# Retention and a squared-ReLU feed-forward net on one core: A11's square on ScalarE, w_out's sums stored in smaller pieces, and transfers held back ahead of the retention products

## The chip, the core and the metric

The kernel runs on one core of a Trainium2 chip, in float32. The metric is device time in microseconds. A core has TensorE (PE in the profile; its weight loads are a row of their own, PEld), VectorE (DVE), ScalarE (ACT), GpSimd (POOL) and SyncE (SP), whose queue issues nearly all transfers here. The engines run their own instruction streams in order and meet at semaphores.

## The reference

```python
q, k, v: (8, 8, 576, 64)           # batch, heads, sequence, head size
scores = q @ k^T / sqrt(64)
Dmat[h, i, j] = gamma[h] ** (i - j) if i >= j else 0
x = ((scores * Dmat) @ v)           # then (batch, seq, heads*64) = (4608, 512)
h = relu(x @ w_in)                  # w_in (512, 2048)
out = (h * h) @ w_out               # w_out (2048, 512), out (4608, 512)
```

The weights may come in as 64-bit floats; the kernel then takes them apart with integer operations on VectorE and ScalarE and puts float32 values together (it calls this rounding).

## The kernel before, in words

**Three strands.** The retention runs over 36 chunks of 128 tokens. The first FFN product runs over 9 blocks of 512 tokens, and its steps are woven between the retention's matmuls. When both are through, a last stage computes the second FFN product from what the first one wrote to DRAM. This last stage is the second part of the span, from about 554 us on.

**The FFN products are done with seven instead of eight block products** (the Strassen-Winograd scheme, `PRODUCTS`, L27). For the first product a block n > 0 has four groups `mp` of seven steps j = 0 to 6, one product each, in `ffn_in` (L723). The products add up in three PSUM banks: h_a (j = 0, 3), h_b (j = 1, 4, 6), h_c (j = 2, 5). A step has four matmuls of 128x128 weights by 256 columns (eight records each of matmuls and weight loads in the trace), and then an ACT or DVE operation that takes the sum out of PSUM:

- j = 0: ACT copies the sum (L748); j = 1 and 2: DVE adds (L750, L752)
- j = 3: ACT applies Relu and makes A11 (L754); POOL multiplies A11 by itself (L755)
- j = 4, 5, 6: DVE adds (L757, L761, L764) and squares (`square`, L745), which makes A22, S3 and A12

A bank that is still read cannot be written, so the matmuls of j = 4 wait for L750, and those of j = 6 for L757. Five results of each group (A11, S1, A12, S3, A22, 256 KB each) go to `g_dram` (`g_store`, L670): A11 in j = 5, A22 in j = 6, and then from a queue of small jobs (`g_sums`, L673, worked off by `some`) A12 in j = 6, S1 and S3 in the next group's j = 0 and 1.

**The retention products** of a chunk are issued by `whole` (L612): 64x64 matmuls, up to 128 of them, that take 2.0 to 2.1 us. They need the transposed q and k of the chunk, which DVE makes block by block (`flip`, L402) and ACT copies in place in 16 small copies (`move`, L421), q scaled (L385) and v scaled (L489) by POOL, and the running state, which ACT copies out of PSUM (L495). After `whole`, the loads of q, k and v for later chunks are issued on SP (`loads`, L867, L155 and L157), and `ffn` (L825) runs the next FFN steps until the pace of a table (`PACE`) is met: seven steps for one chunk in most of the kernel, so that a chunk with its seven steps takes about 14.4 us and its retention products follow j = 6. In `ffn`, `count` is the number of steps still to come before the next retention products. Its flags `held` (the last step) and `busy` (a flip is still to be issued) hold jobs back.

**w_out's preparation** rides along. `w_out_parts` (L259) is a generator of small jobs: 16 pieces of w_out (512 KB each) are fetched (`fetch_w`, L203, three ahead), rounded (`round_parts`, L210: L219, L223 on DVE, L227, L228 on ACT, then L231, L234, L237 on DVE), and summed for the seven products (`right_sums`, L252). A set of sums covers two buffers, `stage[0]` (1.79 MB) and `stage[1]` (1.34 MB), and is stored to `w2_dram` in two transfers (L290). That happens four times. `ffn_in` takes one or two jobs in a step (L780 to L787), at a rate that has all done before block 7 ends; the counter `n_w2` is compared with the steps done.

**The last stage** (from L1138) reads `g_dram` and `w2_dram` back and does the second product block by block, 128x128 matmuls of 128 columns (L1076). Two of its preparations (L1012, L1027 to L1030) run on DVE during the last steps of the first product.

What sets the order around the change is written out by hand: the order of emission is the order of each engine's queue. SP takes transfers strictly in that order, and a transfer whose data is not ready holds up those behind it.

Of the kernel before, what the change touches and what calls it, by code (L numbers as in the profile page):

```python
# [12 lines left out]
AF = mybir.ActivationFunctionType  # L13
ALU = mybir.AluOpType
# [26 lines left out]
def kernel(  # L41
# [33 lines left out]
    nc = tc.nc  # L75
# [8 lines left out]
    N_DF = d_ff // 128  # L84
# [125 lines left out]
    def round_parts(j):  # L210
        words = raw_of(j).bitcast(U32).rearrange("p (n two) -> p n two", two=2)
        lo, hi = words[:, :, 0], words[:, :, 1]
        frac = raw_of(j).rearrange("p (n two) -> p n two", two=2)[:, :, 0]
        exp = exp_of(j).bitcast(U32)
        t = piece_dst(j)
        bits = t.bitcast(U32)

        def one():
            nc.vector.tensor_scalar(exp, hi, 20, 0x7FF, op0=ALU.logical_shift_right, op1=ALU.bitwise_and)  # L219

        def two():

            nc.vector.tensor_scalar(bits, as_dst(j, hi), 0xFFFFF, 0x100000, op0=ALU.bitwise_and, op1=ALU.bitwise_or)  # L223

        def beside():

            nc.scalar.activation(frac, lo, AF.Copy, scale=2.0 ** -52)  # L227
            nc.scalar.activation(exp, exp, AF.Relu, bias=exp_bias[:, 0:1], scale=2.0 ** 23)  # L228

        def three():  # L230
            nc.vector.scalar_tensor_tensor(t, bits, 2.0 ** -20, as_dst(j, frac), op0=ALU.mult, op1=ALU.add)  # L231

        def four():
            nc.vector.tensor_tensor(t, t, as_dst(j, exp_of(j)), op=ALU.mult)  # L234

        def five():
            nc.vector.scalar_tensor_tensor(bits, as_dst(j, hi), 0x80000000, bits, op0=ALU.bitwise_and, op1=ALU.bitwise_or)  # L237

        if not wide:
            to = t if pieces[j][0] == 0 else t.rearrange("p o s f -> p (o s) f")  # L240
            return [lambda: nc.sync.dma_start(to, piece_src(j))] + [lambda: None] * 5
        return [one, two, beside, three, four, five]
# [16 lines left out]
    def w_out_parts():  # L259

        for j in range(N_W1, N_W1 + 3):
            yield lambda j=j: fetch_w(j)
        for j in range(N_W1 + 1, len(pieces), 2):

            pair = [round_parts(j - 1), round_parts(j)]
            for one, two, beside, *_ in pair:
                yield one
                yield two, beside
            for i, (_, _, _, three, four, five) in zip((j - 1, j), pair):
                yield three  # L270
                yield four

                def last(i=i, five=five):
                    five()
                    fetch_w(i + 3)

                yield last
            wi, m, e = pieces[j]
            mh, mq = divmod(m, N_MQ)
            if e == 1:  # L280

                at = slice(2 * mh, 2 * mh + 2)
                b = [stage[0][:, o, at, :] for o in range(4)] + [stage[1][:, o, at, :] for o in range(3)]
                r1, r2, r3, r4 = right_sums(*b)
                yield from (r1, r2, r3, r4)
            if e == 1 and mh == 1:

                for st_, at in ((stage[0], slice(0, 4)), (stage[1], slice(4, 7))):
                    yield from right_sums(*(st_[:, :, o, :] for o in range(NP)))
                    yield lambda st_=st_, at=at, mq=mq: nc.sync.dma_start(  # L290
                        w2_dram[at, :, mq, :].rearrange("o p f -> p o f"), st_.rearrange("p o s f -> p o (s f)"))

    n_made = [0]
    n_raw = [0]
# [428 lines left out]
    def ffn_in(n, mp, j):  # L723

        if j == 0 and mp == 0:

            if n not in sums_x:
                sums_x[n] = sum_x(n)
            for f in sums_x[n]:
                f()  # L730
        left, right, to = PRODUCTS[j]
        if j in OPENS:
            sums[to] = ps_f.tile([128, 2, HT], F32, tag="f", name=f"h_{to}")
        p = sums[to]
        for mm in range(2):
            w = w_in[mp][:, mm, WI_SLOT[left], :, :]
            for c in range(2):
                nc.tensor.matmul(p[:, mm, :], lhsT=w[:, c, :], rhs=xs[n][right][:, c, :],  # L738
                                 start=(j in OPENS and mm == 0 and c == 0), stop=(j in CLOSES and c == 1),
                                 skip_group_check=True)  # L740
        g = g_of(mp)
        p1, u2, p15 = (p_room[mp % 2][:, s, :, :] for s in range(3))

        def square(t):
            nc.vector.scalar_tensor_tensor(t, t, 0.0, t, op0=ALU.max, op1=ALU.mult)  # L745

        if j == 0:
            nc.scalar.copy(p1, p)  # L748
        elif j == 1:
            nc.vector.tensor_tensor(u2, p, p1, op=ALU.add)  # L750
        elif j == 2:
            nc.vector.tensor_tensor(p15, p, p1, op=ALU.add)  # L752
        elif j == 3:
            nc.scalar.activation(g["A11"], p, AF.Relu)  # L754
            nc.gpsimd.tensor_tensor(g["A11"], g["A11"], g["A11"], op=ALU.mult)  # L755
        elif j == 4:
            nc.vector.tensor_tensor(g["A22"], p, p15, op=ALU.add)  # L757
            square(g["A22"])
        elif j == 5:

            nc.vector.tensor_tensor(g["S3"], p, u2, op=ALU.add)  # L761
            square(g["S3"])
        else:
            nc.vector.tensor_tensor(g["A12"], p, p1, op=ALU.add)  # L764
            square(g["A12"])
            queue.extend(g_sums(n, mp))

        if j in (5, 6):
            g_store(n, mp, "A11" if j == 5 else "A22")

        if mp == N_MP - 1 and j in (3, 4, 5) and n_next[0] > n + 1:
            if n + 1 not in sums_x:
                sums_x[n + 1] = sum_x(n + 1)
            sums_x[n + 1].pop(0)()
        if j in (6, 0, 1, 2, 3):
            some(2 if n == 1 and mp == 0 else 1)
        if n == 1 and 1 <= j < 5 and mp + 1 < N_MP:
            sums_w.setdefault(mp + 1, sum_w_in(mp + 1)).pop(0)()

        late_w2 = 0.92 * (done[0] - N_0) - n_w2[0]  # L780
        for _ in range(0 if busy[0] else 2 if late_w2 > 1.5 and j in (0, 3) else late_w2 > 0):
            if not (held[0] and type(w_out_next[0]) is tuple):
                n_w2[0] += 1
                f = w_out_next[0]
                w_out_next[0] = next(w_out_steps, None)
                for f in f if type(f) is tuple else (f,):
                    f and f()  # L787
        if n == N_BLK - 2 and mp == 3 and j in (0, 3):
            assert w_out_next[0] is None
            fetch_w2(j // 3)  # L790
# [4 lines left out]
    w_out_steps = w_out_parts()  # L795
    w_out_next = [next(w_out_steps)]
    held = [False]
    busy = [False]
    n_w2 = [0]

    def block_steps(n):
# [2 lines left out]
            return seconds + [(0, first_in, j) for j in range(N_HALF, N_W1)]  # L804
        return [(n, ffn_in, n, mp, j) for mp in range(N_MP) for j in range(NP)]

    def step():
        n, f, *args = steps.pop(0)
        done[0] += 1
        f(*args)  # L810

    n_next = [0]
    n_scaled = [N_EARLY + 2]
# [11 lines left out]
    def ffn(i, half):  # L825

        gone[0] += C if half == 2 else C / 2
        if steps and steps[0][0] == 0:

            move(6)  # L830
            for _ in range(2 if half and i > N_EARLY else 1):
                if steps and steps[0][0] == 0:
                    convert(6)
                    step()
            return
        if not behind:
            behind.append((gone[0] - HALF, done[0]))
        points = behind + [p for p in PACE if p[0] > behind[0][0]]
        want = points[-1][1]
        for (x0, y0), (x1, y1) in zip(points, points[1:]):  # L840
            if gone[0] < x1:
                want = y0 + (y1 - y0) * (gone[0] - x0) / (x1 - x0)
                break
        count = max(1, int(want) - done[0])
        while steps and count:
            held[0] = half != 1 and count <= (1 if half else 2)

            if half == 2:
                due = sum(m[0] <= i + 2 for m in moves)
                move(max(2, min(4, -(-due // (count - 1)))) if count > 1 else 0)  # L850
            else:
                move(4 if half and len(moves) > 8 else 3 if half else 2 if count > 1 else 0)
            busy[0] = len(flips) > 0
            for f in flips[:1]:
                f()
            del flips[:1]
            step()
            count -= 1
        held[0] = busy[0] = False


    def warm(count):
# [364 lines left out]
```

## Time and profile before

| | |
|---|---|
| median of 3 runs | 954.22 us (953.71 to 954.39) |
| profiled execution | 954.21 us, span of its instructions 952.5 us |
| PE busy | 940.9 us, 99% of the span |
| DVE busy | 777.9 us, 82% |
| ACT busy | 344.0 us, 36%, nearly all of it before 480 us |
| POOL busy | 126.9 us, 13%; L755 has 34.7 of them, L489 51.6, L385 41.0 |
| DMA | 181.43 MB, 190 GB/s over the span |
| stores of the FFN's results | 164 of 256 KB, 3.9 us from issue to landing (median) |
| stores of w_out's sums | 4 of 1792 KB, 6.7 us, and 4 of 1344 KB, 6.1 us |
| fetches of w_out | 16 of 512 KB, 4.6 us |

In the profile "busy" is the time in which an engine has an instruction under way. Matmuls are pipelined and their ends are modelled, so PE's busy time hides small holes, and the starts of its matmuls tell more. A wait row names the engine and line that waited, then what released it. "issue" stands for time in which an engine waited for nothing that the profile shows. PEclk is the granted clock of TensorE as a share of full speed. The page also lists a queue q8 of the kind "instruction", with 76 packets and 1.25 MB.

### The profile page before, as it was taken

How to read it: one execution, taken by the hardware profiler on the slowest of the kernel's cores; microseconds unless marked ns; L12 is line 12 of the kernel's file. 1: busy time of each engine (PE TensorE's matmuls, PEld its weight loads, DVE VectorE, ACT ScalarE, POOL GpSimd, SP SyncE). 2: the span in 40 equal slices, each digit the busy share in tenths (PEclk: the TensorE clock that was granted, in tenths of full speed). 3: DMA queues.
4: the chain of work that ended last, by engine and by line, in shares of the span. 5: the costliest groups of instructions: out<-in, count | busy, mean ns of one | idle time of the engine just before them, and what ended most of it. 6: DMA issues, size and time to landing. Idle time of an engine off the chain costs nothing. (4 is left out here: it accounts for less than half of the span.)

```text
span 952.5 us, 23368 instructions
## 1 busy us (share of the span) xinstructions
PE 940.9 (99%) x9748; PEld 845.9 (89%) x9748; DVE 777.9 (82%) x1422; ACT 344.0 (36%) x812; POOL 126.9 (13%) x115
## 2 busy tenths in 40 slices
PE   8999999999999999999999999999999999999998
PEld 7655888888888888888888899999999999999998
DVE  5789799879898978888856588888878788787876
ACT  4466667567666665766610000000000000000000
POOL 4223131221231312212100000000000000000000
PEclk9999999999999999999999999999999999999999
DMA  9995667695678755863469984535555453525241
GB/s 221 240 287 145 178 187 191 179 283 153 177 210 263 194 154 170 284 183 103 164 201 362 352 294 146 188 129 171 178 157 189 180 182 135 200 100 177 96 172 45
DMA packets 172778, 181.43 MB, mean 190 GB/s; under 512 B 118784, under 2 KB 133248, under 8 KB 166016
## 3 DMA queue, kind: packets, MB, share of 16 engines
q1 hardware_dynamic: 170576, 179.41, 60.6%
q8 instruction: 76, 1.25, 0.6%
q10 hardware_dynamic: 2096, 0.52, 0.3%
q14 instruction: 30, 0.25, 0.1%
HBM read 109.39 MB, written 70.52 MB: 189 GB/s over the span
## 5 line engine op out<-in xcount | busy, mean ns | idle before, releaser
L738 PE MATMUL h_b<-room,w 128*128 128x256 f32 x768 | 182.2, 380 | 2.2 <-DVE room L757 1.9
L421 ACT COPY qk<-flip 32x256 f32<-32x256 f32 x416 | 167.3, 402 | 6.6
L738 PEld LDWEIGHTS h_b<-room,w 128*128 128x128 f32 x768 | 145.8, 190 | 23.4 <-DVE room L757 2.8
L1076 PE MATMUL o_b<-w,room 128*128 128x128 f32 x1168 | 144.4, 275 | 0.2 <-DVE room L1028 0.2
L1076 PEld LDWEIGHTS o_b<-w,room 128*128 128x128 f32 x1168 | 137.3, 192 | 0.4 <-DVE room L1028 0.4
L738 PE MATMUL h_a<-room,w 128*128 128x256 f32 x512 | 125.6, 388 | 1.7 <-issue 1.7
L1076 PE MATMUL o_c<-w,room 128*128 128x128 f32 x1008 | 123.0, 275 | 0.0
L738 PE MATMUL h_c<-room,w 128*128 128x256 f32 x512 | 121.0, 379 | 0.0
L1076 PEld LDWEIGHTS o_c<-w,room 128*128 128x128 f32 x1008 | 117.7, 192 | 0.0
L1090 ACT COPY r<-o_a 128x128 f32<-128x128 f32 x53 | 14.1, 266 | 271.3 <-PE o_a L1076 235.7
L738 PEld LDWEIGHTS h_a<-room,w 128*128 128x128 f32 x512 | 96.0, 191 | 16.1 <-issue 2.2
L738 PEld LDWEIGHTS h_c<-room,w 128*128 128x128 f32 x512 | 97.3, 190 | 13.2
L1076 PE MATMUL o_a<-w,a 128*128 128x128 f32 x688 | 85.6, 275 | 0.0
L755 POOL TENSOR_TENSOR room<-room 128x512 f32<-128x512 f32 x32 | 34.7, 1086 | 361.5 <-ACT room L754 295.9
L1076 PEld LDWEIGHTS o_a<-w,a 128*128 128x128 f32 x688 | 81.2, 192 | 0.1
L745 DVE SCALAR_TENSOR_TENSOR room<-room 128x512 f32<-128x512 f32 x96 | 73.8, 768 | 3.3
L700 PE MATMUL h_ps<-room,w 128*128 128x512 f32 (+2 forms) x160 | 58.8, 516 | 0.7 <-DVE w L237 0.7
L489 POOL TENSOR_TENSOR v_ld<-v_ld,dv 128x512 f32<-128x512 f32 x36 | 51.6, 1435 | 16.4 <-DMA v_ld<-in_v_dram 16.4
L757 DVE TENSOR_TENSOR room<-h_b,room 128x512 f32<-128x512 f32 x32 | 22.0, 689 | 37.6 <-PE h_b L738 37.6
L597 PEld LDWEIGHTS x_ps<-qk,v_ld 64*64 64x64 f32 x1024 | 38.4, 134 | 12.7 <-issue 11.7
L597 PE MATMUL x_ps<-qk,v_ld 64*64 64x64 f32 x1024 | 48.3, 222 | 0.0
L700 PEld LDWEIGHTS h_ps<-room,w 128*128 128x128 f32 x160 | 27.1, 190 | 23.8 <-issue 21.3
(114 smaller groups left out, 1352.2 us busy)
## 6 DMA issues: line engine op xcount, KB each, us to landing
g_dram<-room SPq DMA_DIRECT2D x164, 256.0 KB, 3.9
a<-g_dram SPq DMA_DIRECT2D x30, 1024.0 KB, 6.1
room<-g_dram SPq DMA_DIRECT2D x15, 1024.0 KB, 6.0
w<-w_dram SPq DMA_DIRECT2D x7, 1792.0 KB, 11.2
out_dram<-room SPq DMA_DIRECT2D x17, 512.0 KB, 3.3
q_ld<-in_q_dram SPq DMA_DIRECT2D x64, 128.0 KB, 4.6
w<-in_moe_w_in_dram SPq DMA_DIRECT2D x16, 512.0 KB, 6.2
w<-in_moe_w_out_dram SPq DMA_DIRECT2D x16, 512.0 KB, 4.6
```

Source lines behind the costliest of these rows:

```text
L421: nc.scalar.copy(*moves.pop(0)[2:])
L489: nc.gpsimd.tensor_tensor(vs, vs, dv[:, :, at:at + 1].to_broadcast([C, H, D]), op=ALU.mult)
L597: return [lambda hp=hp, e=e, b=b: nc.tensor.matmul(x_at(hp, e, b, h), lhsT=s["vs"][rows(h), head(hp, e), :], rhs=s["ret"][rows(h), e, hp, ...
L700: nc.tensor.matmul(p, lhsT=w[:, c, :], rhs=xT[0][:, c, :].rearrange("p (h t) -> p h t", h=2)[:, lo:hi, at[0]:at[1]], start=(c == 0), stop= ...
L738: nc.tensor.matmul(p[:, mm, :], lhsT=w[:, c, :], rhs=xs[n][right][:, c, :], start=(j in OPENS and mm == 0 and c == 0), stop=(j in CLOSES a ...
L745: nc.vector.scalar_tensor_tensor(t, t, 0.0, t, op0=ALU.max, op1=ALU.mult)
L755: nc.gpsimd.tensor_tensor(g["A11"], g["A11"], g["A11"], op=ALU.mult)
L757: nc.vector.tensor_tensor(g["A22"], p, p15, op=ALU.add)
L1076: nc.tensor.matmul(p, lhsT=s["lefts"][left][:, m, :], rhs=w_out[j][:, m, WO_SLOT[right], :], start=(i in OPENS and m == 0), stop=(i in CLO ...
L1090: nc.scalar.copy(r[:, 0, 0:128], p)
```

## The change

- A11's square moves from POOL (in j = 3, right after its Relu) to ACT, as an activation at the start of j = 4's work on ACT.
- A22's store is not issued in j = 6 but put on a list, `transfers`, in j = 5. So is each fetch of w_out that follows the rounding of a piece.
- `step` issues one entry of this list after each step (two, if more than two wait), but only if more than `QUIET = 2` steps are still to come before the next retention products (`ahead`; where none follow, it is large).
- A set of w_out's sums is stored in seven transfers of 458 KB, one for each of the seven products. The first four go out beside the four sums of `stage[1]`; the last three are jobs of a new kind (lists), which take no place in the step's count and wait while `ahead` is 2 or less.

The diff, without the places that only set the new variables up:

```diff
                 def last(i=i, five=five):
                     five()
-                    fetch_w(i + 3)
+                    transfers.append((N_BLK, lambda: fetch_w(i + 3)))
...
-                for st_, at in ((stage[0], slice(0, 4)), (stage[1], slice(4, 7))):
-                    yield from right_sums(*(st_[:, :, o, :] for o in range(NP)))
-                    yield lambda st_=st_, at=at, mq=mq: nc.sync.dma_start(
-                        w2_dram[at, :, mq, :].rearrange("o p f -> p o f"), st_.rearrange("p o s f -> p o (s f)"))
+                def keep(o):
+                    nc.sync.dma_start(w2_dram[o, :, mq, :], stage[o // 4][:, o % 4, :, :].rearrange("p s f -> p (s f)"))
+
+                yield from right_sums(*(stage[0][:, :, o, :] for o in range(NP)))
+                for o, r in enumerate(right_sums(*(stage[1][:, :, o, :] for o in range(NP)))):
+                    yield lambda o=o, r=r: [r(), keep(o)]
+                yield [lambda: [keep(4), keep(5)]]
+                yield [lambda: keep(6)]
...
             nc.scalar.activation(g["A11"], p, AF.Relu)
-            nc.gpsimd.tensor_tensor(g["A11"], g["A11"], g["A11"], op=ALU.mult)
         elif j == 4:
+            nc.scalar.activation(g["A11"], g["A11"], AF.Square)
...
-        if j in (5, 6):
-            g_store(n, mp, "A11" if j == 5 else "A22")
+        if j == 5:
+            g_store(n, mp, "A11")
+            transfers.append((n, lambda: g_store(n, mp, "A22")))
...
-        for _ in range(0 if busy[0] else 2 if late_w2 > 1.5 and j in (0, 3) else late_w2 > 0):
-            if not (held[0] and type(w_out_next[0]) is tuple):
-                n_w2[0] += 1
-                f = w_out_next[0]
-                w_out_next[0] = next(w_out_steps, None)
-                for f in f if type(f) is tuple else (f,):
-                    f and f()
+        count = 0 if busy[0] else 2 if late_w2 > 1.5 and j in (0, 3) else late_w2 > 0
+        while w_out_next[0] and (count or type(w_out_next[0]) is list):
+            f = w_out_next[0]
+            if held[0] and type(f) is tuple or ahead[0] <= QUIET and type(f) is list:
+                break
+            n_w2[0] += 1
+            count -= type(f) is not list
+            w_out_next[0] = next(w_out_steps, None)
+            for f in f if type(f) in (tuple, list) else (f,):
+                f()
+            if type(w_out_next[0]) is list:
+                break
...
     def step():
         n, f, *args = steps.pop(0)
         done[0] += 1
         f(*args)
+        for _ in range(2 if len(transfers) > 2 else 1):
+            if transfers and ahead[0] > QUIET:
+                transfers.pop(0)[1]()
...
+            ahead[0] = count
             busy[0] = len(flips) > 0
```

## The prediction

> **What bounds the kernel now.** I read the page first, then PE's waits, then the order of time around each place where PE's matmul starts lie further apart than usual.
>
> ```profile
> PE 940.9 (99%) x9748; PEld 845.9 (89%) x9748; DVE 777.9 (82%) x1422; ACT 344.0 (36%) x812; POOL 126.9 (13%) x115
> ```
>
> TensorE is busy for 99% of the span. The change touches none of its instructions, so it can win only PE's holes, and lose by making new ones. PE's own waits, named by what ended them (us in total, times, longest):
>
> ```profile
> PE h_b L738 <- DVE room L757: 1.9, 2, 1.5
> PE h_a L738 <- issue: 1.7, 1, 1.7
> ...
> PE sc_ps L471 <- ACT qk L421: 0.5, 1, 0.5
> ...
> PE h_b L738 <- DVE room L750: 0.3, 1, 0.3
> PE o_b L1076 <- DVE room L1028: 0.2, 1, 0.2
> ```
>
> These understate the price, since a matmul's modelled end covers part of a hole. I measured the holes by starts: a step j of the first FFN product follows the last one after 1.73 us, or 1.83 after a break. That gives 0.67 us at 112 us, 1.76 at 140, 0.18 at 217.6, 3.58 at 331 to 338, 0.53 at 457.6, 0.72 at 461.8 and 0.48 at 560: **7.9 us** that this change can reach. The start (0 to 98 us) and the last stage are not touched.
>
> The largest hole, in order of time and as stretches (busy us by engine, then PEclk, DMA share, GB/s):
>
> ```profile
> 326.68 0.33 SPq L205 DMA_DIRECT2D w<-in_moe_w_out_dram  x1
> 327.11 6.71 SPq L671 DMA_DIRECT2D g_dram<-room  x3
> ...
> 331.46 0.48 PE L738 MATMUL h_a<-room,w 128*128 128x256 f32 x1
> ...
> 333.62 3.25 PE L738 MATMUL h_a<-room,w 128*128 128x256 f32 x7 [1.67 <-issue]
> ```
> ```profile
> 331.40:333.60 2.20, 0.54 (x9) 0.19 (x1) 2.17 (x5) 2.06 (x5) 0.00 (x0) 1.00 0.17 44
> 333.60:337.10 3.50, 3.48 (x9) 2.77 (x10) 3.50 (x7) 0.21 (x2) 0.00 (x0) 0.52 0.62 163
> ```
>
> PE waits for nothing that the program knows ("issue"), 1.84 us beyond its pitch. After that the granted clock is 0.52 and eight matmul starts lie about 427 ns apart instead of 216: another 1.74. I explain it by PE's own code. Queue q8 of the page carries 76 packets of 16 KB, one for each 256 of PE's instructions, and one of them starts at 331.23, inside the hole. I counted PE's records (matmuls and weight loads) up to each packet. In the quiet last stage packet k starts at record 256 k + 161, some 0.2 us after record 256 k + 158; I call that record the trigger. Here it passes at 325.56 and the packet starts **5.66 us** later, behind a DMA share over 1. In the last two steps before a retention block this hurts: a step eats 16 instructions in 1.73 us, a block some 256 in 2.1 us. PE ran dry some 287 instructions after the trigger, 5.7 us here.
>
> **Change 1: the square of A11 goes from POOL to ACT.** Removed: 32 POOL multiplies (L755, 1.04 us median, 34.7 busy). They slow VectorE whenever it reads two SBUF tensors at the same time:
>
> ```profile
> 458.08 1.55 POOL L755 TENSOR_TENSOR room<-room 128x512 f32<-128x512 f32 x1 [10.35 <-ACT room L754]
> 458.65 1.26 DVE L254 TENSOR_TENSOR w<-w 128x256 f32<-128x256 f32 x1
> ...
> 459.59 1.23 POOL L489 TENSOR_TENSOR v_ld<-v_ld,dv 128x512 f32<-128x512 f32 x1
> 459.94 1.16 DVE L255 TENSOR_TENSOR w<-w 128x256 f32<-128x256 f32 x1
> 461.03 0.68 DVE L757 TENSOR_TENSOR room<-h_b,room 128x512 f32<-128x512 f32 x1
> ...
> 461.76 1.99 PE L738 MATMUL h_b<-room,w 128*128 128x256 f32 x8 [0.46 <-DVE room L757]
> 462.35 0.42 DVE L256 TENSOR_TENSOR w<-w,w 128x256 f32<-128x256 f32 x1
> ```
>
> L254 and L255 need 0.42 alone (L256 below), so the two lose 1.58 us, L757 comes late and PE waits. POOL's scalings of q and v (L385, L489) stood in POOL's queue behind L755, which waits for ACT's Relu. Without it they run as soon as their loads land. The last v load landed at 440, so around 445 to 448 and 458 to 461 POOL is empty: the holes at 457.6 and 461.8 go, **-1.25**. At 140 us the q and v loads landed at 134.2 and 136.4. Both scalings still meet VectorE there, only L755's share goes: between 0 and -0.75 (one slowed operation), I take **-0.3**. At 550.4 L755 lengthens one L1012 by 0.75 in a VectorE run without idle time that ends in PE's wait at 560: **-0.48**.
>
> Added on ACT: 32 squares. The row is the kernel's own L708, and ACT's queue at the first retention block with transposed copies:
>
> ```profile
> L708 ACT ACTIVATE room<-room x14: 612/614/640, 38.8 to 101.2; 128x512 f32<-128x512 f32 x14
> ```
> ```profile
> 105.91 0.60 ACT L754 ACTIVATE room<-h_a 128x512 f32<-128x512 f32 x1 [3.37 <-PE h_a L738]
> 106.53 5.82 ACT L421 COPY qk<-flip 32x256 f32<-32x256 f32 x14
> 112.37 0.37 ACT L495 COPY u_sb<-u_ps 128x256 f32<-128x256 f32 x1
> ```
>
> A square takes 0.61 us, 0.53 in a stream. Behind it on ACT stand the copies of q and k (L421) and the state copy (L495), for which the scores and the next products wait. Mostly ACT then sits idle 0.6 us or more before L495, which hides it; without that cover each block would pay 0.5. At 106.5 to 112.4 there is no idle time and PE already waits: **+0.5**. A11's store on SP now waits for ACT instead of POOL, at about the same moment. **Sum of change 1: -1.5.**
>
> **Change 2: the order of the transfers.** SP's program is in order and waits only for data, so I followed it by the code's own counters. A22's store (256 KB) passes A12's store, the q, k and v loads and S1's store, into the next j = 0, in 25 of 32 cases; the other seven, with more than two steps to go or no block ahead, go out one step earlier than before. Of w_out's 16 fetches (512 KB) 13 go through the list and leave the last two steps, for at most two steps; their consumer comes some nine steps after, so the landing (4.6 us) stays hidden, and would cost PE only once VectorE is late by more than a step. The eight stores of 1.79 and 1.34 MB become 28 of 458 KB: 20 more issues of 0.35 us on SP, which idles. The first four of each seven carry no gate and may still fall into the last two steps.
>
> At 325 us A22's 256 KB leave the queue, and the fetch issued at 326.68 comes a step later (its rounding moves from j = 3 to j = 4), about 328. So the queue should drain near 327 to 328. The packet then comes 2 to 3 us after its trigger, where 3.4 is the limit (5.7 less 1.0 for the packet and 1.3 from its end to the next matmul): **-3.58**.
>
> But the same bytes are now denser right after a block. The other two triggers inside the last two steps while a w_out store drained had no room: 211.4 us (3.67 late, the hole of 0.18) and 402.45 (3.15 late, no hole). There four pieces, up to 1.8 MB, plus A22 now stand where 1.34 MB stood. At about 400 GB/s (402.4 to 405.6) the extra 0.7 MB is 1.8 us at worst, nothing if a packet waits for one piece only. I take **+0.6** for both together, ends 0 and +7 (two holes like the one at 331). At 476.7 up to four pieces and A22 come close to a trigger with 1.9 us to spare: **+0.3**, ends 0 and +1.5.
>
> Two rules of the Trainium skill weigh here. "Runtime: NRT & Kernel Launch", section Instruction fetch mechanics, gives PE 2048 instructions of storage and calls the crossing of a block mostly hidden. By it a packet 5.7 us late costs nothing, the hole is something else, and the change is worth -1.5. The row, a packet inside the hole and PE dry after 287 instructions, speaks for the 512 that the same section has for the other engines; I go by the row. "DMA: Bandwidth & Descriptors", section Bandwidth, wants transfers of 1 MiB and more, and has 78% of the peak there, 32% at 64 KB. An estimate by it, some 60% at 458 KB, makes 1.8 MB cost 1.6 us more, in front of the triggers at 211 and 402. Here 256 KB stores in a row keep the DMA share at 1 at about 400 GB/s, so I take nothing, and keep the rule as the bad case below.
>
> **Sum**: -1.5 - 3.6 + 0.9 = -4.2, rounded to -4. The profiled execution took 954.21 (span 952.5 and 1.7 around it), practically the median of 954.22: **950.2**.
>
> **Rivals and chances.** A (0.46), as summed: 950.2, its own range 948.4 to 952. B (0.24): the hole at 331 goes but one of 2 to 3.6 us opens at 402 or 476, since slack there was under 2 us: 952.5. For it: the denser queue. Against: the smaller pieces. C (0.16), the transfers do not do what they are moved for: the trigger at 325.6 still finds the DMA full, only change 1 counts: 952.7. For it: the fetch of w_out is issued near the trigger also after. D (0.14), the other side: packets at both 211 and 402 come 2 us later than before. A dry spell of 1.7 us brought the half clock, so each costs about 3.6: 950.2 - 0.9 + 7.2 = 956.5. It decides from a delay of 5.3 us after the trigger at both places.
>
> A measurement tells 0.2%, 1.9 us, from no change. Faster by more (under 952.3): 0.44 of A, 0.11 of B, 0.03 of C, so 0.58. Within: 0.02, 0.13, 0.13 and 0.02 of D, so 0.30. Slower: 0.12 of D. The range 948.4 to 956.0 leaves about 0.04 of A and 0.11 of D outside.
>
> **What would show it.** Right: no "issue" wait of PE near 331 and a clock near 1 in every slice; no PE wait for L757 or L750 after 440; one at 112 us grown to about 1.2; no VectorE operation at 458 us over 0.9. Wrong: a 16 KB packet of q8 inside a PE hole at 211 to 218, 402 to 409 or 477 to 483, or PE waiting for L495 or L421 at more blocks than one.

## The result, and the profile after

The changed kernel takes **948.44 us** (median of 4 runs, 947.39 to 949.06); the kernel before, beside it on the same chip, 953.97 (953.08 to 954.39). The ratio is 0.9942, with a 95% interval of 0.9925 to 0.9959: 0.6% faster. The prediction was 950.2, its range 948.4 to 956.0, so the median lies just inside the low end. The profiled execution took 948.65 with a span of 946.93, against 954.21 and 952.49 before. Of all executions below, one (of the transfers alone, 1067.95 us at a mean clock of 0.85) was disturbed and is left aside.

The busy times of the page, and of PE's waits those that answer to the ones shown of before:

```profile
PE 936.9 (99%) x9748; PEld 844.1 (89%) x9748; DVE 764.0 (81%) x1422; ACT 363.2 (38%) x844; POOL 83.6 (9%) x83
```
```profile
PE sc_ps L476 <- ACT qk L426: 1.0, 2, 0.5
...
PE h_b L743 <- DVE room L762: 0.2, 1, 0.2
```

POOL lost its 32 squares (now L761 on ACT), ACT gained them, and VectorE needs 13.9 us less for the same 1422 instructions. The wait named "issue" is gone. The wait for L762 (L757 before) fell from 1.9 to 0.2 us, and the one for ACT's copies (L426, before L421) doubled from 0.5 to 1.0. The waits for L750 and L1028 that before's list had are gone.

The stretches around the former hole at 331 us (us, busy us by engine, PEclk, DMA share, GB/s):

```profile
325.00:328.00 3.00, 3.00 (x15) 2.64 (x15) 2.93 (x5) 2.02 (x5) 0.25 (x1) 1.00 0.50 166
328.00:331.40 3.40, 3.40 (x136) 2.90 (x134) 3.37 (x7) 0.39 (x2) 0.00 (x0) 1.00 0.35 64
331.40:333.60 2.20, 2.20 (x11) 1.94 (x12) 2.17 (x5) 2.14 (x6) 0.00 (x0) 1.00 0.81 293
333.60:337.10 3.50, 3.50 (x18) 3.09 (x17) 3.50 (x7) 3.37 (x9) 0.00 (x0) 1.00 0.67 172
```

PE is busy throughout at clock 1.00. In the two stretches ahead of 331.4 us the DMA share is 0.50 and 0.35, where it was 1.19 and 0.88; the bytes come behind, in the stretches where PE then stood or was slow:

```profile
329.12 0.33 SPq L205 DMA_DIRECT2D w<-in_moe_w_out_dram  x1
329.54 3.46 SPq L676 DMA_DIRECT2D g_dram<-room  x2
```

The fetch of w_out and the next stores of results (L676, L671 before) leave SP at 329.12 and 329.54, where they left at 326.68 and 327.11. The code packet whose trigger passes at 325.48 starts 2.73 us later instead of 5.66.

At 458 us, where VectorE's L254 and L255 took 1.26 and 1.16 us beside POOL:

```profile
456.78 1.67 PE L743 MATMUL h_b<-room,w 128*128 128x256 f32 x7
...
458.10 0.42 DVE L255 TENSOR_TENSOR w<-w 128x256 f32<-128x256 f32 x1
```

L255 takes 0.42 and PE's matmuls follow without a wait.

By stages, from the starts of PE's matmuls (start: up to the first product of h_a; first FFN product: from there to the second product's first; last stage: the rest), the profiled executions differ like this:

| | before | after | difference |
|---|---|---|---|
| start | 98.70 | 99.90 | +1.20 |
| first FFN product, with the retention | 455.98 | 449.42 | -6.56 |
| last stage | 397.81 | 397.61 | -0.20 |
| span | 952.49 | 946.93 | -5.56 |

The change does not touch the start. Over the profiles of kernels with an unchanged start it lasts 98.4 to 100.2 us, so its +1.20 is chance, and the stage in the middle is what I compare below. It repeats well: a second profile of the changed kernel has 449.48.

### The profile page after: what moved, and what is told of

It is laid out like the page before. It is cut to its first block, busy times and chain, and to the rows that moved or that the text cites. A ratio compares the mean times of both kernels' runs of the same rounds, so it can differ in the third digit from the quotient of the medians.

```text
span 946.9 us, 23313 instructions
## 1 busy us (share of the span) xinstructions
PE 936.9 (99%) x9748; PEld 844.1 (89%) x9748; DVE 764.0 (81%) x1422; ACT 363.2 (38%) x844; POOL 83.6 (9%) x83
## 3 DMA queue, kind: packets, MB, share of 16 engines
q8 instruction: 76, 1.25, 0.6%
## 4 chain that ended last, share of the span: by engine, by line
PE 95%; DVE 2%; ACT 1%; DMA 1%; issue 0%; POOL 0%; ACTq 0%; DVEq 0%; POOLq 0%
PE o_b L1096 18%; PE h_b L743 17%; PE h_a L743 12%; PE o_c L1096 12%; PE o_a L1096 12%; PE h_c L743 11%; PE h_ps L705 5%; PE x_ps L602 3%; PE sc_ps L476 2%; PE x_ps L637 1%; PE u_ps L596 1%; DMA v_ld<-in_v_dram 1%; ACT qk L426 1%; DVE w L231 1%; PE t_ps L441 0%
## 5 line engine op out<-in xcount | busy, mean ns | idle before, releaser
L426 ACT COPY qk<-flip 32x256 f32<-32x256 f32 x416 | 167.4, 402 | 6.5
L743 PE MATMUL h_a<-room,w 128*128 128x256 f32 x512 | 123.7, 384 | 0.0
L750 DVE SCALAR_TENSOR_TENSOR room<-room 128x512 f32<-128x512 f32 x96 | 67.2, 700 | 3.3
L390 POOL TENSOR_TENSOR q_ld<-q_ld,dv 128x512 f32<-128x512 f32 x35 | 38.8, 1107 | 288.4 <-DMA q_ld<-in_q_dram 269.4
L494 POOL TENSOR_TENSOR v_ld<-v_ld,dv 128x512 f32<-128x512 f32 x36 | 43.3, 1204 | 64.1 <-DMA v_ld<-in_v_dram 59.3
L762 DVE TENSOR_TENSOR room<-h_b,room 128x512 f32<-128x512 f32 x32 | 22.1, 690 | 32.3 <-PE h_b L743 32.2
```

The source lines that it names most:

```text
L390: engine.tensor_tensor(t, t, dv[:, heads, at:at + 1].to_broadcast(list(t.shape)), op=ALU.mult)
L426: nc.scalar.copy(*moves.pop(0)[2:])
L494: nc.gpsimd.tensor_tensor(vs, vs, dv[:, :, at:at + 1].to_broadcast([C, H, D]), op=ALU.mult)
```

## The experiments

The first four ran on one chip (before there: 952.39, 951.52 to 956.42), the next four on another (before: 953.74, 950.95 to 955.3). My theory was that the hole at 331 is PE's code coming late behind data, that holding transfers back cures it, and that POOL's square costs VectorE time at 140, 458 and 550. The rivals were that POOL and VectorE make the hole at 331 too, or that something else in the denser program does.

**The square alone.** Before, with change 1 only.

```diff
             nc.scalar.activation(g["A11"], p, AF.Relu)
-            nc.gpsimd.tensor_tensor(g["A11"], g["A11"], g["A11"], op=ALU.mult)
         elif j == 4:
+            nc.scalar.activation(g["A11"], g["A11"], AF.Square)
```

> The kernel before with A11's square on ACT and nothing else of the change. Theory (two separate causes: POOL slows VectorE; late blocks of PE's code): the holes at 140, 457.6, 461.8 and 560 shrink or go as in the changed kernel, the one at 112 grows to about 1.2 us, and the one at 331 to 338 (3.6 us, half clock behind it) stays, because the transfers are as before: 951.5, between 951 and 952.5. Rival (the hole at 331 comes of POOL's and VectorE's lateness, not of code): it goes too, about 948.5.

Measured: 952.47 (ratio 0.9992, 0.9977 to 1.0008); middle stage 454.42, so -1.56 where change 1 was put at -1.5. That agreement is luck, as terms that nobody forecast cancel in it. The holes at 457.6, 461.8 and 560 are gone, the one at 140 shrank by 0.62 and the one at 112 grew from 0.67 to 1.34. The hole at 331 stayed: 2.74 us, named "issue", its packet 7.02 us behind the trigger. POOL's square is not its cause. As no slow clock followed it in this execution, it cost 0.89 less than in before, and the retention blocks took 0.87 less (next section). Two things moved against the change: at 218.7 the code hole grew from 0.18 to 1.00, and at 328.9 a new wait of 0.50 opened, where POOL's scalings of q and v, now free to run as soon as their loads land, slowed L660 to 1.55 us (0.68 in before); L237 beside them took 1.43, as beside L755 in before (1.41).

**The transfers alone.** The changed kernel with the square back on POOL.

```diff
             nc.scalar.activation(g["A11"], p, AF.Relu)
+            nc.gpsimd.tensor_tensor(g["A11"], g["A11"], g["A11"], op=ALU.mult)
         elif j == 4:
-            nc.scalar.activation(g["A11"], g["A11"], AF.Square)
```

> The changed kernel with A11's square back on POOL: the transfers' new order and sizes alone. Theory: the holes at 331 and 217.6 go, those at 112 (0.67), 140 (about 1.7), 457 to 462 (1.2) and 560 (0.5) stay: 950.4, between 949.8 and 951.2. The packet of PE's code after 325 us starts about 2.7 us after its trigger, not 5.7. Rival: the hole stays, 953.8.

Measured: 951.94 (ratio 0.9992, 0.9982 to 1.0002), above the 949.8 to 951.2 expected. The middle stage has 452.95, -3.03: the holes at 331 and 217.6 are gone, the packet at 325.62 is 2.76 us late. The holes that belong to POOL stay (0.67 at 112, 1.63 at 140, 0.48 at 558) or grow (454 and 459: 2.01 together, 1.25 before). In this stage the two changes give -1.56 and -3.03 alone and -6.56 together: each alone leaves or opens holes that the other closes.

**Code boundaries moved by 40 records.** Before, with ten small matmuls of 16 columns at the very start (20 more matmuls and 20 more weight loads in the trace). Nothing is moved in the queues; only where the 16 KB boundaries of PE's code fall.

```diff
+        for _ in range(more):
+            nc.tensor.matmul(t[:, 0:16], lhsT=idle, rhs=idle[:, 0:1].to_broadcast([128, 16]), start=True, stop=True)
...
-    warm(5)
+    warm(5, 10)
```

> The kernel before with 10 small matmuls more among the idle ones at the start (40 records of PE more, worked out and thrown away), so that every trigger of PE's code comes 40 records earlier in the program while the transfers stay where they are. Worked out from the trace of before: with a shift of 40 no trigger falls in the last two steps before retention products. Theory (late code): the holes at 331 and 217.6 go and none of this kind opens elsewhere, 950.3 plus what the 10 matmuls cost at the start (under 1.5). Rival (the hole is bound to its place in the program, to its transfers or to the retention data): it stays near 331, 954 or more.

Measured: 952.43 (ratio 1.0002, 0.9986 to 1.0018), but middle stage 452.17, **-3.81**. Step by step and block by block against before, it is the hole at 331 (-3.62) and the one at 217.6 (-0.18), and no other step or block changed by more than 0.05. In order of time:

```profile
328.34 0.33 SPq L205 DMA_DIRECT2D w<-in_moe_w_out_dram  x1
328.76 6.71 SPq L671 DMA_DIRECT2D g_dram<-room  x3
...
333.13 1.78 PE L738 MATMUL h_a<-room,w 128*128 128x256 f32 x7
```

The same fetch and the same 6.71 us of three stores stand ahead of the same product as in before, and PE goes on. The trigger (322.92) now comes 4.3 us earlier against the product, so PE has 9.71 us of code left at it instead of 5.71, and the packet starts 1.54 us after it, before the fetch is issued. This settles that the hole is late code. The gain does not show in the time. In the profiled execution the start is 1.8 us longer (100.54; under 1.5 was expected), with half clock in it (the columns as above):

```profile
8.00:11.50 3.50, 3.50 (x32) 2.85 (x32) 0.93 (x2) 0.58 (x1) 1.85 (x2) 0.51 1.22 272
```

Seven of the other nine executions have the same mean clock, 0.998; where theirs was slow was not recorded. The rest is in the next section, under the slow clock.

**Moved by 100 records.** The same with 25 small matmuls.

```diff
-    warm(5)
+    warm(5, 25)
```

> The same with 25 small matmuls, 100 records. Worked out from the trace of before: the trigger at 331's place has moved off, but one now falls at about 198 us, two steps before retention products and with the DMA full for some 8 us (w_out's store of 1.79 MB). Theory: no hole at 331; a new one of 1 to 3.5 us between 200 and 206, with 'issue' as its name, perhaps half clock behind it: 951 to 955, and the profile shows it. Next to no room also at about 389 and 270. Rival: the hole stays near 331 and none comes near 202.

Measured: 959.46 (ratio 1.0073, 1.0058 to 1.0088). All of the loss is in the start, 107.16 us, with one stall of 2.2 us and a slow clock from 7.8 to 18 us; the middle stage is 452.16, -3.82. The hole at 331 went as forecast. The new hole that I forecast near 202 to 206 did not come: that packet is 3.32 us late, and PE's code lasted just so long. I had read the queue there as fuller than it was.

**The changed kernel once more**, unchanged, on the second chip.

> The changed kernel once more, beside the kernel before on the same chip as the next three. The kernel before had the half clock behind its hole in only some of its executions on the chip of the last runs (median 952.4, five of 25 above 953.6), so the ratio should lie nearer 0.996 than 0.994: 948.4, stage of the first product 449.4 in the profile.

Measured: 948.42 (ratio 0.9949, 0.9934 to 0.9964), middle stage 449.48, the packets at 211, 325, 398 and 471 us late by 2.88, 2.72, 2.76 and 1.01.

**Nothing held back.** The changed kernel, its transfers still on the list and in pieces, but issued at once.

```diff
-    QUIET = 2
+    QUIET = 0
```

> The changed kernel with QUIET = 0: smaller pieces and ACT's square stay, but nothing is held back ahead of the retention products; A22's store goes out in j = 5, the fetches of w_out in the step that orders them. If holding back is what cures the hole at 331: the fetch near 326.7 and A22's store stand in front of the packet again, 5 to 7 us after its trigger, a hole of 1.5 to 3.6 there: 950 to 952. If the smaller pieces do it: no hole, 948.4.

Measured: 951.75 (ratio 0.9988, 0.9974 to 1.0001), middle stage 3.65 longer than the changed kernel's. The hole at 331 is back with 2.27 us, the packet 5.83 late. So the pieces alone do not cure it. The other 1.4 are at 140 us, which the order of time explains (below).

**Whole stores.** The changed kernel with w_out's sums stored in two transfers of 1.79 and 1.34 MB again, fetches and A22 held back as before.

```diff
-                def keep(o):
-                    nc.sync.dma_start(w2_dram[o, :, mq, :], stage[o // 4][:, o % 4, :, :].rearrange("p s f -> p (s f)"))
...
+                for st_, at in ((stage[0], slice(0, 4)), (stage[1], slice(4, 7))):
+                    yield from right_sums(*(st_[:, :, o, :] for o in range(NP)))
+                    yield lambda st_=st_, at=at, mq=mq: nc.sync.dma_start(
...
```

> The changed kernel with w_out's sums stored as before, in two transfers of 1.79 and 1.34 MB; the holding back and ACT's square stay. If holding back is the cure at 331: no hole there, or one under 1 us, since w_out's fetch falls a step earlier than in the changed kernel; at 211 and 402 the packets come about 3 to 4 us after their trigger as before, holes of 0 to 1: 948.4 to 950. If the smaller pieces do it: a hole of 1.5 to 3.6 at 331, 950 to 952.

Measured: 950.80 (ratio 0.9976, 0.9963 to 0.9989), middle stage 2.57 longer than the changed kernel's. Holes of 0.99 at 217.2 and 1.45 at 332.5, packets 4.80 and 5.07 late; the second lies between the two forecasts. So holding back alone does not do it either; this kernel needs both halves of change 2. Only the hole at 217 speaks of the size: there the 1.34 MB store leaves SP 0.8 us ahead of the trigger, and the packet comes when the queue has drained. At 332 the schedule moved as well: w_out's fetch leaves SP at 326.25 and a store at 326.68, 1.1 and 1.5 us after the trigger, where they leave at 329.12 and 329.54 in the changed kernel.

**The copies ahead of the first such block.** The changed kernel, with up to 16 copies put on ACT before each step of one call of `ffn` instead of 2, against the wait at 112 us (1.34 us as counted here, 1.27 in the expectation).

```diff
-                move(4 if half and len(moves) > 8 else 3 if half else 2 if count > 1 else 0)
+                move(16 if i == N_ONE and half == 0 else 4 if half and len(moves) > 8 else 3 if half else 2 if count > 1 else 0)
```

> The changed kernel with one number changed: ahead of the first retention products with transposed copies (ffn with i == N_ONE and half == 0) ACT issues up to 16 of the copies of q and k before each step instead of 2. ACT idles 3.4 us in front of A11's Relu there, and 12 to 14 copies then stand in one row with the square in front of the scores. Theory: the copies move into the idle time, the hole at 112 (1.27 in the changed kernel) goes to under 0.2, 947.2; if the copies wait for VectorE's transposes instead of for their turn, nothing changes.

Measured: 953.35 (ratio 1.0001, 0.9990 to 1.0012), 5 us slower than the changed kernel. The wait at 112 is gone, but PE waits 4.4 us inside the same block, with a slow clock behind it. ACT in order of time:

```profile
109.94 0.60 ACT L759 ACTIVATE room<-h_a 128x512 f32<-128x512 f32 x1
110.57 0.63 ACT L761 ACTIVATE room<-room 128x512 f32<-128x512 f32 x1
111.10 6.59 ACT L426 COPY qk<-flip 32x256 f32<-32x256 f32 x16
117.72 0.37 ACT L500 COPY u_sb<-u_ps 128x256 f32<-128x256 f32 x1
```

After the 15 copies that belong to this block, my edit put 16 of the next block's in front of the state copy L500, which ends at 118.09; PE goes on at 118.16. The page names another releaser (POOL's v scaling, which ended at 118.00), but in the changed kernel PE passed that place at 114.7 us, before this scaling had begun (116.04), so it cannot be what was needed. The edit was too broad; the idea of bringing only that block's own copies forward was not tried.

## Why the prediction was right, and which terms were off

The sum had -4.2, the profiled executions show -5.56. The gain was larger than that: the middle stage and the last stage have -6.76, and the start's +1.20, which is chance, hides part of it. Without it the profiled execution would have come to about 947.5, below the range; that the number came out inside is partly luck. By its terms:

| step | predicted | measured |
|---|---|---|
| hole at 331 to 338 | -3.58 | -3.63 |
| 457.6 and 461.8 | -1.25 | -1.25 |
| 560 | -0.48 | hole gone; last stage -0.20 |
| 112, ACT's row | +0.5 | +0.67 |
| 140 | -0.3 (0 to -0.75) | **-1.29** |
| 211 and 402, denser queue | +0.6 (0 to +7) | -0.18 |
| 476.7 | +0.3 (0 to +1.5) | 0 |
| retention blocks | 0 | **-0.87** |
| start | 0 | +1.20, chance |

**331.** Right in mechanism, and in size against an execution of before with the slow clock (1.74 of the 3.58; see below). Change 2 brings the drain to 327 to 328 us, and the packet comes 2.73 us after its trigger (2 to 3 forecast). The limit of 3.4 us held in all the kernels. Packets asked for in the last two steps before a retention block, where PE had between 5.5 and 6.3 us of code left at the trigger (not all: those left out came at most 3.31 us after it and made no hole):

| kernel, trigger at | packet after it | hole |
|---|---|---|
| after, 325.5 | 2.73 | 0 |
| after, 398.3 | 3.07 | 0 |
| before, 402.5 | 3.15 | 0 |
| 100 records, 206.8 | 3.32 | 0 |
| before, 211.4 | 3.67 | 0.18 |
| square alone, 211.8 | 4.43 | 1.00 |
| whole stores, 210.1 | 4.80 | 0.99 |
| whole stores, 325.2 | 5.07 | 1.45 |
| before, 325.6 | 5.66 | 1.84 and the slow clock |
| nothing held back, 325.9 | 5.83 | 2.27 |
| square alone, 326.5 | 7.02 | 2.74 |

With 6.3 us of code left, 3.67 us did no harm (changed kernel, 138.3). In all seven holes PE stopped behind the same record, number 290 after the trigger (the prediction had some 287), and went on 2.2 to 2.5 us after the packet's start. The packet can also come behind what is issued after its trigger: in the four traces with a hole at 331 the fetch left SP 1.1 to 1.8 us after the trigger (1.1 in before), and the packet came behind it.

The Trainium skill ("Runtime: NRT & Kernel Launch", section Instruction fetch mechanics) calls crossing a block of code mostly hidden; I went by the row, and the table with the run of 40 moved records supports that.

**211, 402 and 476.7.** The reserve of +0.9 was not needed. The four pieces that may fall into the last two steps did not delay the packets: 2.95 us at 211.6 (3.67 before), 3.07 at 398.3, 1.29 at 471.1. The mis-sized term is the fear of a denser queue; I had charged it 0.6 of the 1.8 us that the extra bytes could cost if they all stood in front of the packet. But there was little to spare: at 398.3 the 291st record came at 404.25, 0.4 to 0.7 us after the moment at which that packet (401.38) would have let PE go on, by the 2.2 to 2.5 us of the holes. The rule of the Trainium skill ("DMA: Bandwidth & Descriptors", section Bandwidth) for transfers of 1 MiB and more spoke against the pieces. Here the pieces landed in 4.6 us (median), and with whole stores (6.1 to 6.7 us in before) the kernel was slower by 2.4, in part because of the moved fetch. At 211 the pieces keep the DMA share at 1.03 up to 215.5, and the packet starts at 214.50 all the same; with the whole stores it starts at 214.86, when the share has fallen from 0.97 to 0.1. So a full queue alone does not keep a packet out; what decides when it comes, no run here settles.

**140.** This is the term that failed, beyond its bound of -0.75. I had reasoned that both scalings "still meet VectorE there" and that only L755's share of 0.75 could go. In order of time:

```profile
134.89 1.22 POOL L390 TENSOR_TENSOR q_ld<-q_ld,dv 128x512 f32<-128x512 f32 x1 [6.97 <-DMA q_ld<-in_q_dram]
...
135.43 0.69 DVE L757 TENSOR_TENSOR room<-h_c,room 128x512 f32<-128x512 f32 x1 [0.24 <-PE h_c L743]
...
137.06 1.18 POOL L494 TENSOR_TENSOR v_ld<-v_ld,dv 128x512 f32<-128x512 f32 x1 [0.95 <-DMA v_ld<-in_v_dram]
...
137.24 1.55 DVE L249 TENSOR_TENSOR w<-w 128x512 f32<-128x512 f32 x1
...
140.77 1.56 PE L743 MATMUL h_b<-room,w 128*128 128x256 f32 x6 [0.20 <-DVE room L762]
```

The q scaling L390 meets L757, which reads a PSUM bank and one SBUF tensor, and L757 takes its usual 0.69. Only L249, with two SBUF inputs, is slowed, to 1.55. Before, two such operations were (L231 1.53, L234 1.43). The Trainium skill has this rule ("SBUF — State Buffer", section SBUF: two separate sides: VectorE contends with GpSimd when it has two SBUF inputs); I had used it at 458 us, but at 140 I counted scalings instead of asking which operation each one would meet. How much it depends on the moment shows in the run with nothing held back, where the loads land 0.7 us later:

```profile
135.62 1.61 POOL L390 TENSOR_TENSOR q_ld<-q_ld,dv 128x512 f32<-128x512 f32 x1 [7.77 <-DMA q_ld<-in_q_dram]
...
136.22 1.55 DVE L237 SCALAR_TENSOR_TENSOR w<-w,w 128x512 uint32<-128x512 uint32 x1
...
138.29 1.54 DVE L231 SCALAR_TENSOR_TENSOR w<-w,w 128x512 f32<-128x512 uint32 x1
```

Now both scalings meet an operation with two SBUF inputs, and the hole at 141 us is 1.74 instead of 0.36. In the changed kernel's second profile the hole is 0.41, so it repeats for one program. A good part of this gain is still where the loads happened to land, and the bound should have reached to about -1.6, the whole hole.

**112.** The queue on ACT was read right, and the term is 0.17 short: ACT runs without a pause from 107.1 to 114.2 us, and PE waits twice.

```profile
107.11 0.60 ACT L759 ACTIVATE room<-h_a 128x512 f32<-128x512 f32 x1 [3.37 <-PE h_a L743]
107.73 0.82 ACT L426 COPY qk<-flip 32x256 f32<-32x256 f32 x2
108.57 0.63 ACT L761 ACTIVATE room<-room 128x512 f32<-128x512 f32 x1
109.23 4.99 ACT L426 COPY qk<-flip 32x256 f32<-32x256 f32 x12
114.25 0.37 ACT L500 COPY u_sb<-u_ps 128x256 f32<-128x256 f32 x1
```

**Retention blocks.** Sixteen blocks take 2.08 us instead of 2.13. That was not in the sum. It comes with the square's move (it is there with the square alone, not with the transfers alone). Inside each of them PE waits for ACT's state copy (L495, now L500), which starts 0.82 us after the block's first matmul in before and 0.76 after. In before most of these copies have a separate wait instruction on ACT ahead of them:

```profile
L495 ACTq EVENT_SEMAPHORE  x40: 17/17/17, 27.5 to 482.0; - x40
L500 ACTq EVENT_SEMAPHORE  x1: 17/17/17, 27.5 to 27.5; - x1
```

There are 40 of them in before and with the transfers alone, and 1 in the changed kernel and with the square alone. Where before has none ahead of the block's copy (the blocks at 185, 315, 448 and 480), the copy starts at 0.76 and the block takes 2.08 there too. So the program lost a wait instruction that cost 0.05 us a block. That the square, which itself waits on ACT, had made this second wait needless is likely, but not shown.

**The slow clock.** I counted 1.74 us of the hole at 331 as half clock that always follows. It does not: of 25 runs of before on the first chip, 20 took at most 953.1 us at a mean clock of 0.999 or more, and five 953.7 to 956.4 at 0.998 or less; on the second chip 15 of 29 and 14. A stretch of half clock as in the profile (3.5 us at 0.52) takes 0.002 off the mean. On the first chip before was therefore nearer to 952.4, which is part of why the single parts and the moved boundaries show so little in the medians while their stages show 1.6 to 3.8 us. None of the changed kernel's ten executions was below 0.999, and they all lie between 947.2 and 949.1: against an execution of before without the slow clock the change is worth some 4 us, against one with it some 6.

## What to carry to other kernels

A hole of PE named "issue" is to be laid against the instruction queue's packets: a late code packet shows as one inside the hole, and moving the code boundaries by a few idle matmuls tells it apart from everything else without touching the schedule. Read this in the stage, not in the time, since the added matmuls can cost something of their own. Where it is that, keep the DMA queue short at the triggers whose code runs out fast (here a stretch of many small matmuls), by holding transfers back and by cutting the large ones. Beside POOL, ask of each VectorE operation whether it reads two SBUF tensors, and at which moment it will run, rather than how many POOL operations there are.

## What the runs showed of the hardware that I had not expected

- The half clock does not follow from the length of a stop alone. In the profiled executions the hole of 1.84 us at 331 in before brought PEclk 0.52 behind it, and longer ones, 2.27 (nothing held back) and 2.74 (the square alone), brought none. The mean clocks say that it differs between executions of one kernel (14 of 29 of before on the second chip, 5 of 12 with nothing held back).
- A packet of code of 16 KB can wait 5 to 7 us behind data (5.66 in before, 7.02 with the square alone), in four traces behind a fetch that left SP 1.1 to 1.8 us after its trigger too, while the same queue elsewhere serves it 0.1 to 1 us after its trigger.
- Ten matmuls of 16 columns at the start came with half clock from 8.1 us on and a start of 100.54 us, and twenty-five with half clock from 7.8 to 18 us and a start of 107.16, against full clock there in before and starts of 98.4 to 100.2.
- A separate wait instruction ahead of an ACT copy delayed the copy by 0.05 us, and with it PE, in sixteen blocks.
